# Moving the squares and RMS scales of a fused attention and SwiGLU kernel ahead of its loads, and leaving all engines but TensorE to a list scheduler

## The chip, the core and the metric

One core of one Trainium2 chip. The time is the device time of one execution in microseconds (us). A run's state is noted: it is called slow here when it is over 1.5% above the fastest run of the same kernel, and fast runs are compared with fast runs. The profiled span is about 1.7 us shorter than the reported time of the same execution.

Engines are named as in the profile: PE is TensorE (matmuls and transposes), PEld its weight loads, DVE VectorE, ACT ScalarE, POOL GpSimd, SP SyncE.

## What is computed

```python
# q, k, v: [8, 8, 576, 64] (batch, head, position, head dim); s: [8, 8, 576]
scores = (1 / 8) * q @ k^T + min(-(cum[i] - cum[j]), 0)   # cum = cumsum(max(s, 0)); causal
x = softmax(scores) @ v                                   # then [batch * position, 512]
xn = x / sqrt(mean(x * x) + 1e-6) * rms_g                 # RMS norm of each token
out = (silu(xn @ w_gate) * (xn @ w_val)) @ w_out          # 512 -> 1536 -> 512, 4608 tokens
```

## The kernel before

There are eight batches of 576 tokens in the attention, and nine chunks of 512 tokens in the feed-forward network (FFN). The kernel's main loop alternates them. `attention(b)` has eight units (a pair of heads and a part of the positions each). `ffn1(c)` is the gate and value matmuls of chunk c: twelve groups of 16 matmuls of 256 columns (8 of 512 in the later chunks), each into one of two PSUM buffers `psD`, followed by Silu on ACT and a product on DVE (`H_sb`). The second product, `ffn2_steps(c)`, is woven into the next attention. Three more words: a pack is a DVE copy that reorders a loaded q or k of batch 0 or 1 for its transposes; weighting v is POOL's product of v with the decay weights; a mask is POOL's instruction that makes `E` causal. Where an engine is said to stand, it is idle until something it waits for is done.

`ffn1` also takes fillers: small jobs with a place between 0 and 1, issued between its groups. In the kernel before they include the end of the previous attention: squares of blocks 2 to 4 of `x_blk` (ACT, with sums), the RMS scale `al` from those sums (POOL), the scaling (DVE) and the transposes into `psX` (PE).

```python
def att_square(a, tb):                                    # ACT
    nc.scalar.activation(out=sq_scr[:, 0:DM], in_=a.x[:, tb, :], func=AF.Square,
                         accum_out=a.ss[:, tb : tb + 1])
def att_alpha(a, t0, t1):                                 # POOL
    ... al = (ss / DM + 1e-6) ** -0.5 ...
def att_scale(a, tb):                                     # DVE
    ... a.x[:, tb, :] *= al[:, tb] ...
def att_out(a, tb):                                       # PE: x_blk -> psX; DVE: psX * g -> xnT
    ...
def tail_fillers(a, lo, hi):
    fns = [lambda tb=tb: att_square(a, tb) for tb in (2, 3, 4)]
    fns += [lambda: att_alpha(a, 2, 5)]
    fns += [lambda tb=tb: (att_scale(a, tb), att_out(a, tb)) for tb in (2, 3, 4)]
    return spread(fns, lo, hi)

def attention(b, filler, lead, each):
    ... # units; each: PE scores -> ACT exp (E) -> POOL causal mask -> PE psAV -> DVE x_blk
    ... # squares, al and scale of blocks 0 and 1 after units 4 and 6
    return a

with tc.manual_schedule():          # every engine runs in program order
    ... # loads and preparation of batch 0 (cut)
    a = attention(0, iter(()), (0, 0, 0), 0)
    load_runs(1, 0)                 # k of batch 1, issued by POOL
    load_runs(1, 1)                 # q of batch 1
    load_w(2, 0, 6)                 # w_out in two halves
    load_w(2, 6, 12)
    load_v(1, nc.gpsimd)            # v of batch 1, five loads
    for c in range(NCH):
        fillers = []
        if c < B:
            fillers += tail_fillers(a, 0.0, 0.25 if c == 0 else 0.4)
        ... # preparation of batch c + 1: packs (DVE), transposes, norms (ACT), v weighting (POOL)
        if c + 2 < B:
            for w in range(2):      # ten POOL issues: k and q of batch c + 2
                fillers.append((0.1, lambda b=c + 2, w=w: load_kq(b, w)))
            fillers.append((0.1, lambda b=c + 2: load_v(b, nc.sync)))
        if c == B:
            check_decay()           # checks of the input's range, before the last FFN
            check_all()
        Ht = ffn1(c, quarters if c == 0 else halves if c < 4 else whole, fillers)
        fl = ffn2_steps(c, Ht)
        if c + 1 < B:
            a = attention(c + 1, fl, (8, 4, 6), 3)
        else:
            for _ in fl:
                pass
... # a slow general path for inputs that fail the checks (cut)
```

## Time and profile before

| | before |
|---|---|
| time, us | 505.26 median of 2 runs (503.77 to 506.76) |
| profiled span, us | 504.7 |
| PE busy | 395.9 us, 78% of the span |
| PE waiting at `psX` for scaled `x_blk` | 77.5 us, 25 times, the longest 32.4 |
| mean granted PE clock | 0.925 of full speed |

First the page of the kernel before: busy time by engine, and the span in 40 equal slices of 12.6 us (a digit is tenths of busy time; PEclk is the granted clock in tenths).

```profile
PE 395.9 (78%) x3083; PEld 226.9 (45%) x3083; DVE 230.7 (46%) x461; ACT 215.1 (43%) x351; POOL 172.3 (34%) x267
...
PE   3740068697799779986998699959995999697995
...
PEclk9985559999899989998999899989998999998898
DMA  9999950019701980199019901990110011002002
```

PE works 78% of the time, and in slices 4 and 5 (counted from 1, 37.9 to 63.1 us) it does nothing at all, while the DMA engines are full (digit 9; 189 GB/s over these 25 us). The clock digit is 5 there and in the slice after. Who made PE wait is in the list of PE's waits (what it waited for: total us, times, longest):

```profile
PE psX L330 <- DVE x_blk L323: 77.5, 25, 32.4
PE psT L201 <- DVE xnT L191: 7.8, 7, 1.7
```

Most of it is one cause: transposes of `x_blk` that wait for the scaling on DVE (77.5 of the 108.8 us in which PE is not busy). The timeline of PE in the first FFN shows the long one (columns: start, duration, what; in brackets the idle time before it and what ended it):

```profile
31.34 1.04 PE L345 MATMUL psD<-xnT,wv_sb 128*128 128x256 bf16 x8
64.78 0.61 PE L330 MATMUL psX<-ident_bf,x_blk 128*128 128x128 bf16 x4 [32.40 <-DVE x_blk L323]
65.18 1.91 PE L345 MATMUL psD<-xnT,wg_sb 128*128 128x256 bf16 x8
```

PE stops at 32.4 and goes on at 64.8. The scaling waited for `al` on POOL, as DVE's timeline shows:

```profile
63.59 1.13 DVE L323 TENSOR_SCALAR x_blk<-x_blk,al 128x512 bf16<-128x512 bf16 x1 [29.00 <-POOL al L320]
```

POOL's timeline tells why `al` came so late:

```profile
29.18 2.68 POOL L118 DMA_DIRECT2D v_nat<-in_v_dram  x3
35.22 0.89 POOL L118 DMA_DIRECT2D v_nat<-in_v_dram  x1 [3.37 <-DMA wv_sb<-in_moe_w_val_dram]
...
43.93 0.89 POOL L105 DMA_DIRECT2D k_nat<-in_k_dram  x1 [3.86 <-DMA xnT<-in_q_dram]
...
59.88 2.43 POOL L105 DMA_DIRECT2D q_nat<-in_q_dram  x3 [0.36 <-DMA v_nat<-in_v_dram]
62.39 0.20 POOL L318 TENSOR_SCALAR al<-ss 128x3 f32<-128x3 f32 x1
```

POOL issues 19 loads between attention 0 and `al` (L318): k, q, two halves of w_out, five of v, then five each of k and q of batch 2. From the fourth load of v on it stands before nearly every one until an earlier load has landed. In the lines shown that is the eighth before it: the first `k_nat`, the tenth of the row, is released by the second, `in_q_dram`, after 3.86 us. The issue itself takes only 0.9 us, and its end in the record is not the landing of the load: the issue of 0.77 us for q of batch 1 landed 16.4 us after its start.

In later stages the same chain is shorter. In the second FFN, PE's timeline reads:

```profile
121.82 1.04 PE L345 MATMUL psD<-xnT,wv_sb 128*128 128x256 bf16 x8
125.50 0.61 PE L330 MATMUL psX<-ident_bf,x_blk 128*128 128x128 bf16 x4 [2.64 <-DVE x_blk L323]
125.90 1.91 PE L345 MATMUL psD<-xnT,wg_sb 128*128 128x256 bf16 x8
...
130.92 0.40 PE L330 MATMUL psX<-ident_bf,x_blk 128*128 128x128 bf16 x4 [1.68 <-DVE x_blk L323]
```

PE waits 2.64 and 1.68 us (a third wait, of 1.68, ends at 134.74). After the first, the matmuls run at about half speed: eight matmuls of 256 columns take 1.91 us and not 1.04. After the two waits of 1.68 us they take 1.04 and 1.05.

### The profile page before, as it was taken

The page shows a single profiled execution, that of the slowest core. Times are in us where ns is not written, and L with a number is a line of the kernel's source. Part 1 is how long each engine was busy: PE and PEld are TensorE (multiplying, and loading weights), DVE is VectorE, ACT ScalarE, POOL GpSimd, SP SyncE. Part 2 cuts the span into 40 slices and gives each one's busy share as a digit, 9 for nine tenths or more (in the row PEclk, how much of TensorE's full clock was granted, in tenths as well). Part 3 has the DMA queues.
Part 4 walks back from the last instruction along what each step waited for, and adds up shares of the span by engine and source line. Part 5 has one row for each costly group of instructions (what it writes and reads, how often), then busy time and mean ns, then how long its engine had stood idle before and what let it go on. Part 6 is the DMA issues. An engine that isn't in the chain of part 4 may idle for free.

```text
span 504.7 us, 7722 instructions
## 1 busy us (share of the span) xinstructions
PE 395.9 (78%) x3083; PEld 226.9 (45%) x3083; DVE 230.7 (46%) x461; ACT 215.1 (43%) x351; POOL 172.3 (34%) x267
## 2 busy tenths in 40 slices
PE   3740068697799779986998699959995999697995
PEld 2530047545584558455844254425442544243442
DVE  6730035565336634563355435643564356433331
ACT  2830006583257425751565156615652566120220
POOL 8651540049204930393039403940224022000000
PEclk9985559999899989998999899989998999998898
DMA  9999950019701980199019901990110011002002
GB/s 151 199 197 195 183 26 0 2 43 153 78 0 43 144 88 2 43 129 101 1 43 121 109 0 44 113 117 1 38 46 1 0 44 44 0 1 83 1 2 88
DMA packets 97803, 33.75 MB, mean 67 GB/s; under 512 B 85856, under 2 KB 92512, under 8 KB 97760
## 3 DMA queue, kind: packets, MB, share of 16 engines
q0 software_dynamic: 63840, 16.52, 34.5%
q1 hardware_dynamic: 33920, 16.67, 14.0%
q8 instruction: 26, 0.43, 0.3%
q14 instruction: 17, 0.14, 0.1%
HBM read 37.90 MB, written 9.44 MB: 94 GB/s over the span
## 4 chain that ended last, share of the span: by engine, by line
PE 57%; DMA 12%; POOL 10%; DVE 9%; ACT 8%; issue 4%; SPq 0%; ACTq 0%; POOLq 0%
PE psD L345 35%; PE psO L373 11%; DMA v_nat<-in_v_dram 8%; PE psT L211 4%; PE psX L330 3%; DMA xnT<-in_k_dram 3%; DVE H_sb L352 3%; ACT S_sb L351 3%; DVE x_blk L323 2%; POOL al L320 2%; POOL q_nat L105 2%; PE psAV L301 2%; ACT E L277 2%; POOL E L279 2%; PE psD L272 2%
## 5 line engine op out<-in xcount | busy, mean ns | idle before, releaser
L351 ACT ACTIVATE S_sb<-psD 128x512 bf16<-128x512 f32 x108 | 64.3, 595 | 240.1 <-PE psD L345 239.7
L352 DVE TENSOR_TENSOR H_sb<-S_sb,psD 128x512 bf16<-128x512 bf16 x108 | 74.2, 687 | 165.1 <-ACT S_sb L351 165.1
L345 PE MATMUL psD<-xnT,wg_sb 128*128 128x256 bf16 (+1 forms) x624 | 121.9, 335 | 0.0
L345 PE MATMUL psD<-xnT,wv_sb 128*128 128x256 bf16 (+1 forms) x624 | 118.3, 327 | 0.0
L279 POOL TENSOR_SCALAR_AFFINE_SELECT E<-E 128x512 bf16<-128x512 bf16 x64 | 41.1, 642 | 213.1 <-ACT E L277 212.9
L373 PE MATMUL psO<-wout_sb,H_sb 128*128 128x512 bf16 x432 | 107.4, 379 | 0.0
L345 PEld LDWEIGHTS <-wv_sb 128*128 128x128 bf16 x624 | 64.1, 103 | 38.0 <-issue 5.3
L330 PE MATMUL psX<-ident_bf,x_blk 128*128 128x128 bf16 x160 | 17.4, 238 | 77.6 <-DVE x_blk L323 77.5
L345 PEld LDWEIGHTS <-wg_sb 128*128 128x128 bf16 x624 | 60.1, 104 | 30.9 <-issue 2.8
L277 ACT ACTIVATE E<-psD 128x1024 bf16<-128x1024 f32 x64 | 63.6, 1023 | 8.0 <-PE psD L272 7.7
L373 PEld LDWEIGHTS <-H_sb 128*128 128x128 bf16 x432 | 36.9, 98 | 34.9 <-issue 3.0
L330 PEld LDWEIGHTS <-x_blk 128*128 128x128 bf16 x160 | 10.6, 104 | 90.6 <-DVE x_blk L323 87.6
L378 DVE COPY osb<-psO 128x512 f32<-128x512 f32 x36 | 24.8, 688 | 29.1 <-PE psO L373 29.1
L301 PE MATMUL psAV<-vw,E 128*128 128x65 bf16 x576 | 32.3, 199 | 6.2 <-POOL E L279 4.3
L237 POOL TENSOR_TENSOR vw<-v_nat,wT 128x512 bf16<-128x512 f32 (+1 forms) x35 | 35.5, 1044 | 0.0
L301 PEld LDWEIGHTS <-E 128*128 128x128 bf16 x576 | 23.6, 100 | 20.1 <-POOL E L279 10.7
L323 DVE TENSOR_SCALAR x_blk<-x_blk,al 128x512 bf16<-128x512 bf16 x40 | 18.9, 489 | 29.8 <-POOL al L320 29.3
L306 DVE TENSOR_TENSOR x_blk<-psAV,rZ 128x256 bf16<-128x256 f32 (+1 forms) x64 | 31.4, 491 | 2.2
L334 DVE TENSOR_TENSOR xnT<-psX,g_sb 128x512 bf16<-128x512 bf16 (+1 forms) x40 | 24.8, 636 | 14.3 <-PE psX L330 13.7
L105 POOL DMA_DIRECT2D k_nat<-in_k_dram x30 | 25.8, 880 | 12.2 <-DMA wout_sb<-in_moe_w_out_dram 7.7
L272 PE MATMUL psD<-QT,KT 64*128 64x256 bf16 (+2 forms) x320 | 26.7, 266 | 0.9 <-ACT E L277 0.9
L105 POOL DMA_DIRECT2D q_nat<-in_q_dram x30 | 25.4, 901 | 1.6 <-DMA v_nat<-in_v_dram 1.6
(80 smaller groups left out, 289.9 us busy)
## 6 DMA issues: line engine op xcount, KB each, us to landing
out_dram<-osb SPq DMA_DIRECT2D x36, 256.0 KB, 2.0
v_nat<-in_v_dram SPq DMA_DIRECT2D x24, 256.0 KB, 9.7
k_nat<-in_k_dram POOLq DMA_DIRECT2D x24, 128.0 KB, 4.5
q_nat<-in_q_dram POOLq DMA_DIRECT2D x24, 128.0 KB, 7.9
v_nat<-in_v_dram POOLq DMA_DIRECT2D x8, 256.0 KB, 16.0
wg_sb<-in_moe_w_gate_dram POOLq DMA_DIRECT2D x2, 768.0 KB, 14.8
wv_sb<-in_moe_w_val_dram POOLq DMA_DIRECT2D x2, 768.0 KB, 18.6
wout_sb<-in_moe_w_out_dram POOLq DMA_DIRECT2D x2, 768.0 KB, 22.7
```

Source lines behind the costliest of these rows:

```text
L105: nc.gpsimd.dma_start(out=dst[0:n, b % 2, sc, :, :], in_=src[b, :, sc * 128 : sc * 128 + n, :].rearrange("h p d -> p h d"))
L237: eng.tensor_tensor(out=vw[0:n, sc, :, 0:64], in0=v_nat[0:n, b % 2, sc, :, :], in1=wb.unsqueeze(2).to_broadcast([n, H, D]), op=ALU.mult)
L272: nc.tensor.matmul(st[:, j, c0 : c0 + q1 - q0], lhsT=KT[rs, hp, kb * 128 : kb * 128 + 128], rhs=QT[rs, hp, q0:q1], start=(i == 0), stop=(i ...
L277: nc.scalar.activation(out=E, in_=st, func=AF.Exp, scale=0.125)
L279: nc.gpsimd.affine_select(out=diag, in_=diag, pattern=[[0, 4], [1, 128]], compare_op=ALU.is_ge, fill=0.0, base=0, channel_multiplier=-1)
L301: nc.tensor.matmul(AV[:, j, qb - q0, :], lhsT=E[:, j, c0 : c0 + 128], rhs=vw[:, kb, h, :], start=(j == 0 and i == 0), stop=(j == 1 and i = ...
L306: nc.vector.tensor_tensor(out=a.x[:, q0 : q0 + nq, hp * 128 : (hp + 1) * 128].rearrange("p t (j d) -> p j t d", j=2), in0=AV[:, :, :, 0:64 ...
L330: nc.tensor.matmul(X[:, cc, :], lhsT=a.x[:, tb, cc * 128 : (cc + 1) * 128], rhs=ident_bf, is_transpose=True, start=(cc == 0), stop=(cc == ...
L345: nc.tensor.matmul(P[:, j, i * n : (i + 1) * n], lhsT=w[:, cc, fb * 128 : (fb + 1) * 128], rhs=xnT[:, cc, t0 + o : t0 + o + n], start=(i = ...
L351: nc.scalar.activation(out=sl, in_=P[:, 0, :], func=AF.Silu)
L352: nc.vector.tensor_tensor(out=Ht[:, f0 : f0 + m, o : o + n], in0=sl.rearrange("p (i n) -> p i n", i=m), in1=P[:, 1, :].rearrange("p (i n) ...
L373: nc.tensor.matmul(O, lhsT=Ht[:, fb, tb * 128 : (tb + 1) * 128], rhs=wout_sb[:, fb, :], start=(fb == 0), stop=(fb == FB - 1))
```

## The change

The intent is to take the chain squares, scale factor, scaling out of the FFN: its squares, `al` and scaling of blocks 2 to 4 are issued at the end of `attention`, ahead of the next loads, and only the transposes stay in the FFN. In the same step the program order is kept on PE alone. On the other engines a list scheduler now orders the instructions at build time (it changes their order on each engine, not what they do).

```diff
-    def tail_fillers(a, lo, hi):
-        fns = [lambda tb=tb: att_square(a, tb) for tb in (2, 3, 4)]
-        fns += [lambda: att_alpha(a, 2, 5)]
-        fns += [lambda tb=tb: (att_scale(a, tb), att_out(a, tb)) for tb in (2, 3, 4)]
-        return spread(fns, lo, hi)
+    def tail_fillers(a, steps):
+        return [(p, lambda tb=tb: att_out(a, tb)) for p, tb in zip(steps, (2, 3, 4))]
@@ attention
             take(filler, each)
+        for tb in (2, 3, 4):
+            att_square(a, tb)
+        att_alpha(a, 2, 5)
         if each:
             for tb in (0, 1):
                 att_out(a, tb)
             for _ in filler:
                 pass
+        for tb in (2, 3, 4):
+            att_scale(a, tb)
         return a
@@
-    with tc.manual_schedule():
+    with tc.manual_schedule(engines={mybir.EngineType.PE}):
@@
-                fillers += tail_fillers(a, 0.0, 0.25 if c == 0 else 0.4)
+                fillers += tail_fillers(a, (0.08, 0.16, 0.24) if c == 0 else (0.16, 0.25, 0.33))
```

## The prediction

> **What bounds the kernel now.** 505.26 us; TensorE (PE) is busy 395.9 of 504.7 us (part 1 of the page). By the list of waits PE waits 77.5 us in 25 gaps at the transposes into psX for the scaled x_blk. One gap is 32.4 us (timeline, 32.4 to 64.8): the RMS scale of blocks 2 to 4 (POOL al) stands on POOL behind the next batches' loads, whose issues wait for earlier loads to land; DMA is saturated there (about 190 GB/s in the stage table). In each later stage (50 to 51 us) the same chain costs PE about 2.6+1.7+1.7 us, and afterwards a group of 16 matmuls at the half clock takes 3.3 instead of 1.8 us.
>
> **What the change does.** No work is added or removed. The order of instructions shows:
> 1. Squares and scale of blocks 2 to 4 stand before the FFN; in the first batch the scale now follows three of the v loads instead of all remaining issues. In later stages it follows the v weighting (4 blocks at 1.01 us) and precedes the k/q loads, which go to the end of the FFN.
> 2. New hazard: on VectorE (DVE) the pack of q of batch 1 stands in attention 0, before unit 5's normalisation. It waits for a load that landed at 43.2 us (issue 26.8 + 16.4), behind the same saturated queue. [...] so attention 0 stands until 43 to 44.
> 3. In later attentions the scaling of blocks 0 and 1 stands before unit 5's normalisation and waits for POOL, which has one weighting block (1.01 us) more between the masks. Loss.
> 4. After the attention ACT does 3 squares, two norms (1.2 us each) and the table load (1.28 us) before the first Silu. The third FFN group waits for that and for H_sb behind xnT on DVE.
> 5. The decay checks leave the last FFN's front.
>
> **Sum, from durations in the trace.**
> - Start: q lands 43.5; packs, units 5 and 6, scales, transposes, unit 7 to 49.3; group 0 (cold, 3.7) 53; Silu, square, scale on POOL (behind one 0.9 us issue) 56.5; group 1 from 57.3; group 3 from 66 (before 72.5); nine groups at 1.8, eight transposes at 0.43, a cold group: FFN 0 ends about 87.5, before 99.6. Its pack-to-transpose waits (4 x 1.5 us) vanish. Gain 12.
> - Stages 1 to 5: the transposes' waits and the cold group (about 7) go; attention +2.0, one PE wait of about 1.8 before group 2: gain about 3.2 each, 16. Stages 6 and 7: 3.2 + 2.7.
> - Last FFN: PE waits 3.6 us for the checks, 1.6 remain: gain 2.
>
> Total about 36: **predicted 469 us**, 80% range 459 to 481. Faster by over 2%: 0.96; within 2%: 0.03; slower: 0.01.
>
> **What would show it.** The 32.4 us gap becomes one of about 20 us (24 to 44), released by DVE packing q; then about 4 us at the first psX. FFN 0 ends at 86 to 89. Stages 1 to 5 last about 48 us; their FFN starts 2 us later after the attention's start, PE's waits for x_blk near zero, about 1.8 at group 2.
>
> **What would make it wrong.** q landing much earlier or later; ACT's norms delaying the first Silu until PE goes cold in every stage (1.5 us each, 10 in all); masks delayed by k/q issues at the start of an attention; the clock.

That attention 0 stands until 43 to 44 was my assumption; the trace of the kernel after shows such a stand (below). The sum comes to about 36 us.

## The result, and the profile after

| | before | after |
|---|---|---|
| time, us (2 runs each) | 505.26 (503.77 to 506.76) | 457.78 (457.10 to 458.46) |
| profiled span, us | 504.7 | 455.4 |
| PE busy, us | 395.9 | 379.5 |
| mean granted PE clock | 0.925 | 0.989 |

The ratio is 0.906, 95% interval 0.8931 to 0.9189. Ratios here are the mean time of one kernel's fast runs over the mean of the other's fast runs of the same rounds, so they are not quite the ratios of the medians quoted. The kernel is 47 us faster, predicted were 36: the time fell 1.2 us below the range's lower end of 459.

The same lines of the page, after (a slice is now 11.4 us):

```profile
PE 379.5 (83%) x3083; PEld 222.8 (49%) x3083; DVE 225.7 (50%) x461; ACT 217.3 (48%) x351; POOL 171.4 (38%) x267
...
PE   1640599988988899879986998889988998999994
...
PEclk9999989999999999999999999999999999999998
DMA  8999999450092409850594019100110011002002
```

One hole is left in PE's line (slice 4, 34 to 46 us). The clock digits are 8 and 9 throughout, but this record is too kind just after the hole. By stretches (columns: window, its length, busy time and number of instructions of PE, PEld, DVE, ACT, POOL; granted clock, DMA share, GB/s):

```profile
46.00:52.00 6.00, 5.10 (x36) 3.69 (x36) 2.79 (x7) 2.28 (x5) 0.00 (x0) 1.00 1.22 218
56.00:60.00 4.00, 3.69 (x25) 2.90 (x26) 2.48 (x7) 2.48 (x6) 4.00 (x5) 0.58 0.90 124
```

From 46 to 52 us a clock of 1.00 is recorded, and yet eight matmuls take 1.90 us there, as at half speed (PE's timeline below, 48.56). The record and the durations disagree here, and I go by the durations. PE's waits:

```profile
PE psX L330 <- DVE x_blk L323: 22.8, 2, 18.7
PE psD L345 <- DVE H_sb L352: 11.5, 6, 1.9
PE psAV L301 <- DVE x_blk L306: 10.0, 7, 1.5
...
PE psAV L301 <- POOL E L279: 7.1, 5, 1.7
```

The 77.5 us at `psX` fell to 22.8, of which 18.7 are one wait. Three rows that are new or larger stand out: waits for `H_sb` before an FFN group (11.5), for `x_blk` (10.0) and for the mask `E` (7.1) before a `psAV`. The timeline of PE in the start:

```profile
26.37 1.50 PE L301 MATMUL psAV<-vw,E 128*128 128x65 bf16 x24
46.55 1.03 PE L330 MATMUL psX<-ident_bf,x_blk 128*128 128x128 bf16 x8 [18.68 <-DVE x_blk L323]
...
48.56 1.90 PE L345 MATMUL psD<-xnT,wg_sb 128*128 128x256 bf16 x8
...
56.30 0.60 PE L330 MATMUL psX<-ident_bf,x_blk 128*128 128x128 bf16 x4 [4.14 <-DVE x_blk L323]
56.70 1.91 PE L345 MATMUL psD<-xnT,wg_sb 128*128 128x256 bf16 x8
...
62.24 1.03 PE L345 MATMUL psD<-xnT,wg_sb 128*128 128x256 bf16 x8
```

PE now stands inside attention 0, from 27.87 to 46.55, and then 4.14 us for `al`. DVE's timeline shows what the first stand is:

```profile
43.99 0.36 DVE L191 COPY xnT<-xnT 96x768 bf16<-96x768 bf16 x1 [17.28 <-DMA xnT<-in_q_dram]
44.27 0.18 DVE L305 RECIPROCAL rZ<-psAV 128x6 f32<-128x6 f32 x1
```

The scheduler put the packing of q of batch 1 (L191) before attention 0's normalisation of unit 5 (L305, L306), and it waits for its load. The instructions behind it did not pass: PE had ended its `psAV` matmuls at 27.87, and yet the reciprocal that reads them (L305) started only behind the pack, at 44.27. DVE was idle for 17.28 us meanwhile.

To see where the 49.3 us of span lie, I cut both spans at the first FFN matmul and the first `psO` matmul of each chunk, read from PE's timeline:

| stretch, us | before | after | difference | predicted |
|---|---|---|---|---|
| start to first FFN matmul | 27.67 | 48.56 | +20.9 | |
| FFN 0 | 71.93 | 31.45 | -40.5 | |
| together: start to end of FFN 0 | 99.60 | 80.01 | -19.6 | -12 |
| attentions 1 to 5 | 89.25 | 103.07 | +13.8 | +10 |
| FFN 1 to 5 | 166.67 | 136.53 | -30.1 | -26 |
| attentions and FFN 6 and 7 | 94.98 | 86.58 | -8.4 | -5.9 |
| FFN2 of chunk 7 with the checks, last FFN | 37.49 | 32.52 | -5.0 | -2 |
| tail | 16.71 | 16.69 | 0.0 | |
| sum | 504.7 | 455.4 | -49.3 | -36 |

FFN 1 to 5 gained 6.0 us each, 33.3 to 27.3 in the mean: the waits for `x_blk` and the cold matmuls (those at about half speed, 1.91 us for eight of 256 columns) are gone; in FFN 1 to 5 of the kernel after, every such row takes 1.02 to 1.05 us. The attentions lost: attention 2 takes 22.1, numbers 3 to 5 take 20.6, numbers 1, 6 and 7 take 19.0, all of them 17.9 before. In attention 2 PE's timeline reads:

```profile
131.29 0.39 PE L272 MATMUL psD<-QT,KT 64*128 64x256 bf16 x4
133.40 0.36 PE L301 MATMUL psAV<-vw,E 128*128 128x65 bf16 x6 [1.72 <-POOL E L279]
```

and POOL's in the same stretch:

```profile
124.87 4.31 POOL L105 DMA_DIRECT2D k_nat<-in_k_dram  x5 [23.29 <-ACT S_sb L351]
129.14 3.54 POOL L105 DMA_DIRECT2D q_nat<-in_q_dram  x4
132.62 0.72 POOL L279 TENSOR_SCALAR_AFFINE_SELECT E<-E 128x512 bf16<-128x512 bf16 x1
```

The first mask (L279) starts as the ninth POOL issue of k and q loads for a later batch ends; the scheduler put them in front. Its input was ready some 1.5 us before (ACT's three exps began at 130.04 and take 0.95 each). PE waits 1.72 us.

In the FFN, the new wait comes from ACT: in FFN 2 the squares, two norms (L231) and the loading of the Silu table stand before the first Silu, and the third group waits for a free `psD`:

```profile
151.17 1.04 PE L345 MATMUL psD<-xnT,wv_sb 128*128 128x256 bf16 x8
...
154.34 0.93 PE L345 MATMUL psD<-xnT,wg_sb 128*128 128x256 bf16 x7 [1.91 <-DVE H_sb L352]
```

```profile
150.50 1.06 ACT L231 ACTIVATE sq_scr<-k_nat 128x1024 bf16<-128x1024 bf16 x1
...
151.67 1.28 ACT L351 ACT_TABLE_LOAD   x1
152.97 1.09 ACT L351 ACTIVATE S_sb<-psD 128x512 bf16<-128x512 f32 x2
```

So the profile suggests that the new source order gains much, and that the scheduler's order gives part of it back: at the pack of q (DVE), at the masks (POOL), at the norms (ACT). That is a reading, and the experiments test it.

### The profile page after: what moved, and what is told of

It is laid out like the page before. It is cut to its first block, busy times and chain, and to the rows that moved or that the text cites. A ratio compares the mean times of both kernels' runs of the same rounds, so it can differ in the third digit from the quotient of the medians.

```text
span 455.4 us, 7760 instructions
## 1 busy us (share of the span) xinstructions
PE 379.5 (83%) x3083; PEld 222.8 (49%) x3083; DVE 225.7 (50%) x461; ACT 217.3 (48%) x351; POOL 171.4 (38%) x267
## 4 chain that ended last, share of the span: by engine, by line
PE 51%; issue 11%; POOL 11%; ACT 10%; DVE 8%; DMA 7%; POOLq 0%; ACTq 0%
PE psD L345 33%; PE psO L373 10%; DMA xnT<-in_q_dram 6%; POOL E L279 5%; PE psT L211 3%; DVE x_blk L306 3%; ACT sq_scr L313 3%; ACT E L277 2%; ACT sq_scr L231 2%; PE psD L272 2%; DVE x_blk L323 1%; POOL vw L237 1%; POOL q_nat L105 1%; POOL al L320 1%; DVE osb L378 1%
## 5 line engine op out<-in xcount | busy, mean ns | idle before, releaser
L351 ACT ACTIVATE S_sb<-psD 128x512 bf16<-128x512 f32 x108 | 63.8, 596 | 130.0 <-PE psD L345 128.6
L345 PE MATMUL psD<-xnT,wg_sb 128*128 128x256 bf16 (+1 forms) x624 | 113.5, 318 | 11.7 <-DVE H_sb L352 11.5
L345 PE MATMUL psD<-xnT,wv_sb 128*128 128x256 bf16 (+1 forms) x624 | 112.7, 316 | 0.0
L345 PEld LDWEIGHTS <-wv_sb 128*128 128x128 bf16 x624 | 61.8, 99 | 33.4
L345 PEld LDWEIGHTS <-wg_sb 128*128 128x128 bf16 x624 | 57.2, 99 | 39.3 <-issue 12.5
L279 POOL TENSOR_SCALAR_AFFINE_SELECT E<-E 128x512 bf16<-128x512 bf16 x64 | 41.3, 653 | 85.2 <-ACT E L277 84.9
L313 ACT ACTIVATE sq_scr<-x_blk 128x512 bf16<-128x512 bf16 x40 | 25.1, 627 | 51.0 <-DVE x_blk L306 50.5
L301 PE MATMUL psAV<-vw,E 128*128 128x65 bf16 x576 | 30.8, 202 | 18.1 <-DVE x_blk L306 10.0
L301 PEld LDWEIGHTS <-E 128*128 128x128 bf16 x576 | 23.5, 102 | 31.9 <-DVE x_blk L306 13.5
L330 PE MATMUL psX<-ident_bf,x_blk 128*128 128x128 bf16 x160 | 16.1, 227 | 25.6 <-DVE x_blk L323 22.8
L306 DVE TENSOR_TENSOR x_blk<-psAV,rZ 128x256 bf16<-128x256 f32 (+1 forms) x64 | 31.3, 489 | 1.9
L305 DVE RECIPROCAL rZ<-psAV 128x4 f32<-128x4 f32 (+1 forms) x64 | 11.7, 183 | 36.8 <-PE psAV L301 36.8
L323 DVE TENSOR_SCALAR x_blk<-x_blk,al 128x512 bf16<-128x512 bf16 x40 | 14.9, 408 | 28.1 <-POOL al L320 28.1
L330 PEld LDWEIGHTS <-x_blk 128*128 128x128 bf16 x160 | 11.3, 101 | 34.0 <-DVE x_blk L323 23.5
## 6 DMA issues: line engine op xcount, KB each, us to landing
wv_sb<-in_moe_w_val_dram POOLq DMA_DIRECT2D x2, 768.0 KB, 18.8
wout_sb<-in_moe_w_out_dram POOLq DMA_DIRECT2D x2, 768.0 KB, 22.6
```

What stands on the lines that cost most here:

```text
L279: nc.gpsimd.affine_select(out=diag, in_=diag, pattern=[[0, 4], [1, 128]], compare_op=ALU.is_ge, fill=0.0, base=0, channel_multiplier=-1)
L301: nc.tensor.matmul(AV[:, j, qb - q0, :], lhsT=E[:, j, c0 : c0 + 128], rhs=vw[:, kb, h, :], start=(j == 0 and i == 0), stop=(j == 1 and i = ...
L306: nc.vector.tensor_tensor(out=a.x[:, q0 : q0 + nq, hp * 128 : (hp + 1) * 128].rearrange("p t (j d) -> p j t d", j=2), in0=AV[:, :, :, 0:64 ...
L345: nc.tensor.matmul(P[:, j, i * n : (i + 1) * n], lhsT=w[:, cc, fb * 128 : (fb + 1) * 128], rhs=xnT[:, cc, t0 + o : t0 + o + n], start=(i = ...
L351: nc.scalar.activation(out=sl, in_=P[:, 0, :], func=AF.Silu)
```

## The experiments

The theory: the moved squares and scales bring the whole gain, and the list scheduler costs time in three separate places, one for each engine. The rival: both halves belong together, and the scheduler brings part of the gain (for example, by placing `al` and the loads better than the source does). Each run is compared with the kernel before on the same chip (medians of before: 504.80, 504.54 and 503.99 us in the three sessions). The variants of the scheduler are one line each. They are correct, as all runs here are.

### The two halves of the change

The new source with every engine in program order:

```diff
-    with tc.manual_schedule(engines={mybir.EngineType.PE}):
+    with tc.manual_schedule():
```

> The changed source (squares and scales in front of the loads), program order kept on all engines. Theory M (all of the gain comes from the moved squares and scales; the list scheduler takes part of it back, by packing q inside attention 0 and by issuing loads in front of the masks): 433 us (428 to 440), faster than the changed kernel by about 25; FFN 0 starts at about 28 us as in the kernel before instead of 48.6, attentions last 17.9 us as before, FFNs 27 to 28. Rival R (the scheduler's order brings most: packs, peaks and checks out of the way): 475 to 490, slower than the changed kernel.

Measured: 421.78 us median of five runs, 420.40 of the three fast ones; ratio of the fast runs 0.8332 (0.8295 to 0.8369). That is 37 us faster than the kernel after, fast runs with fast runs. The runs fell in two groups, 420.1 to 421.8 and 427.0 to 427.3 (slow); this comes up again below. The run takes the edit of the source as a whole: that it is the chain moved ahead of the loads, and not the new places of the transposes, is read from PE's waits for scaled `x_blk` (77.5 us before, 4.0 in e1's second profile); no run took the two apart.

The old source with the scheduler:

```diff
# in the kernel before
-    with tc.manual_schedule():
+    with tc.manual_schedule(engines={mybir.EngineType.PE}):
```

> The source of before, order kept on PE only. On POOL the scale of blocks 2 to 4 of batch 0 stays behind all loads, but in later stages the scheduler puts it in front of them. Theory M: 465 us (459 to 475): the stall at the start ends at about 65 us as before, FFN 0 ends near 88 us, later stages as in the changed kernel. Rival R': the source part is needed in every stage, then 485 to 500.

Measured: 477.33 us (476.40 to 477.77, four runs); ratio 0.9451 (0.9422 to 0.9480). I had expected 465. In later stages the scheduler alone does move `al` ahead of the loads (after attention 1 `al` of blocks 2 to 4 starts at 108.20 and the loads of k at 134.52; before, the loads were first) and so heals part of the old order. In the first batch it does not: `al` starts at 61.86, as late as before (62.39). PE still waits 30.1 us for scaled `x_blk`; 18.1 of them are the same stand in attention 0 as in the kernel after, the other 12.0 are for this `al`.

What follows: the halves overlap. From the old source, the scheduler gains 27 us. From the new source, it loses 37 us. The rival is right about the first and wrong about the kernel at hand: with the source order mended, the scheduler of all four engines costs far more than it gains. In this sense the theory, "the whole gain is the source's", stands; how much of the 47 us one ascribes to each half depends on which is put in first.

### Which engine's order costs what

One engine more is given back its program order, from the kernel after:

```diff
-    with tc.manual_schedule(engines={mybir.EngineType.PE}):
+    with tc.manual_schedule(engines={mybir.EngineType.PE, mybir.EngineType.DVE}):    # e3
+    with tc.manual_schedule(engines={mybir.EngineType.PE, mybir.EngineType.Pool}):   # e4
```

> The changed kernel with program order kept on DVE too. Theory M: the 18.7 us wait in attention 0 is DVE standing at the pack of q, so it goes: FFN 0 starts at 28 us, PE then waits at the first psX until about 38, FFN 0 ends at 68 to 70; then the masks of attention 1 stand behind the k/q loads of batch 3 on POOL until about 78, so only 4 to 8 us remain of it: 450 us (445 to 455). Rival: attention 0 stands for another reason (DMA or POOL), FFN 0 starts at 45 or later and the time stays at 456 to 460.

> The changed kernel with program order kept on POOL too. Theory M: the extra time of attentions 2 to 5 (20.6 to 22.1 us against 19.0 for 1, 6, 7) is the k/q loads issued on POOL in front of the masks; with them back in the FFN these attentions last 19 us or less, 7 to 9 us less in all, and as the scheduler then places the pack of q after attention 0, FFN 0 starts before 32 us: 437 us (431 to 444). Rival (DVE's and ACT's order make the attentions long): attentions 2 to 5 stay above 20 us.

Measured: 448.75 us with DVE in order (447.37 to 452.22, ratio 0.8872, 0.8842 to 0.8902) and 437.08 with POOL in order (436.35 to 440.63, ratio 0.8642, 0.8615 to 0.8668). Both are as expected in time; in e3 partly by luck, since FFN 0 was expected to end at 68 to 70 and ended at 79.2. With DVE in order, FFN 0 starts at 28.98 and not at 48.56: the stand of 18.7 us was DVE's order. But FFN 0 then takes 50.2 and not 31.5 us, so the start as a whole gains only 0.8 us: in program order DVE does the packs of batch 1 shortly before PE needs them, PE waits four times for them (1.68, 1.84, 5.09 and 2.04 us) and 5.15 us for `al`, and the granted clock over FFN 0 is 0.77. This profile is the slowest of e3's five runs, 3.5 us above their median, and the wait of 5.09 belongs to a long pack of the kind told below; what the start gains without it, no profile shows. With POOL in order FFN 0 ends at 63.8 us, and attentions 2 to 5 take 18.8 to 19.1. Attention 1 takes 24.2, however: POOL weights v of batch 1 (65.45 to 70.48) only after it has issued all loads of k and q of batch 2, and the masks come behind it.

Next, all but one engine in order:

```diff
+    with tc.manual_schedule(engines={mybir.EngineType.PE, mybir.EngineType.DVE, mybir.EngineType.Pool}):          # e6: ACT scheduled
+    with tc.manual_schedule(engines={mybir.EngineType.PE, mybir.EngineType.Activation, mybir.EngineType.Pool}):   # e7: DVE scheduled
```

> The changed kernel with program order kept on PE, DVE and POOL: against e1_source_only only ACT's order (and SP's) is the scheduler's. Theory A (the wait of 1.9 us at the third group of each FFN is ACT: two norms stand before the first Silu): FFNs 27.2 to 27.6 us as in the changed kernel, attentions 17.7 to 17.9 as in e1; 430 to 433 us, about 10 more than e1_source_only. Rival D (it is H_sb behind xnT on DVE): FFNs 25.7, time within 2 us of e1_source_only.

> The changed kernel with program order kept on PE, ACT and POOL: against e1_source_only only DVE's order (and SP's) is the scheduler's. Theory A: FFNs 25.7 as in e1. The scaling of blocks 0 and 1 in front of later normalisations costs 0.5 to 1.2 us per attention (18.3 to 19.0), the early decay checks save 5.0 us at the last FFN (11.8 + 20.7 against 14.0 + 23.6), the early packs of batch 1 shorten FFN 0 from 42 to about 33 us while attention 1 then waits for its v weights as in e4_pe_pool (24 us). Together about e1_source_only: 418 to 425 us. Rival D: FFNs above 27.

Measured: with ACT alone scheduled 437.91 us (437.67 to 441.87, ratio 0.8674, 0.8612 to 0.8736), some 17 more than the fast runs with all in order; I had expected 430 to 433. In its profile the two packs took 4.35 us at 64.49, the slow case of the two that are told below, so its start (72.9 us) is to be compared with e1's slow run (70.2 us) and not with the column beside it. With DVE alone scheduled 416.33 (414.37 to 417.56, ratio 0.8226, 0.8170 to 0.8281), the fastest up to then and below the 418 to 425 expected: attention 1 took 19.2 us and not 24.

| stretch, us | after: all but PE scheduled | e3: POOL, ACT scheduled | e4: DVE, ACT scheduled | e6: ACT scheduled | e7: DVE scheduled | e1 again: none scheduled |
|---|---|---|---|---|---|---|
| start to end of FFN 0 | 80.0 | 79.2 | 63.8 | 72.9 | 61.5 | 63.3 |
| attention 1 | 19.1 | 18.5 | 24.2 | 18.7 | 19.2 | 17.9 |
| attention 2 | 22.1 | 19.3 | 18.8 | 17.9 | 17.9 | 17.9 |
| attentions 3 to 5, mean | 20.6 | 19.9 | 19.0 | 17.9 | 17.9 | 17.9 |
| FFN 1 to 6, mean | 27.3 | 27.4 | 27.5 | 27.6 | 25.7 | 25.7 |
| FFN2 of chunk 7, checks | 11.8 | 13.9 | 11.8 | 14.0 | 11.8 | 13.9 |

("e1 again" is the second profile of e1, below. The starts of e3 and e6 hold a long pack. The order of SP, which issues loads and stores, is the scheduler's in all columns but that of e1 again.) The table gives each engine its part:

- ACT's order costs 1.9 us in each of FFN 1 to 5 (27.4 to 27.2 in e6, 25.5 to 25.3 in e1 again). Every column with ACT scheduled has 27 to 28 us in the mean, both without it have 25.7. In e6, where ACT alone is scheduled, PE's waits show the same row as after (11.5 us there):

```profile
PE psD L345 <- DVE H_sb L352: 11.6, 6, 2.0
```

- POOL's order costs 1.4 to 3.3 us in each of attentions 2 to 5: they are long where POOL is scheduled (after, e3) and 17.9 to 19.1 where it is in order. In both runs ACT was scheduled too. Another 0.9 to 1.2 us are a matter of their own: they are there when DVE and ACT are both scheduled (e4), and gone with either alone (e6, e7). They go with PE's seven waits for `x_blk` before a `psAV` (10.0 us after and in e4; no such row in e3, e6 and e7): DVE has the scaling of blocks 0 and 1, which waits for POOL's `al` (2.14 us at 143.47 in the kernel after), before a normalisation. This is item 3 of the prediction.
- DVE's order alone costs nothing in the attentions (I had expected 0.5 to 1.2 us each: a miss) and gains 2.1 us at the checks, part of which it takes off the critical path, and 1.4 in the last FFN (22.1 to 20.7), where the matmuls then start at full speed (four of 512 columns take 1.04 us, and 1.89 in the kernel before). The 17.3 us stand of DVE at the pack of q is not in e7, where FFN 0 starts at 29.75, nor in e3 and e4: it goes when either DVE or POOL is given its order back. (In every run that has it, ACT was scheduled too.) Why the scheduler places the pack so early only then, no run shows.

So "one separate place for each engine" was too simple. ACT's cost in the FFN stands alone (e6); POOL's in the attentions was seen only beside ACT's order, as no run scheduled POOL alone; the stand in the start and the 0.9 to 1.2 us in the attentions need at least two engines' orders together.

### Does the start hang on q's landing?

The load of q is issued before that of k, in the kernel after:

```diff
-        load_runs(1, 0)
         load_runs(1, 1)
+        load_runs(1, 0)
```

> The changed kernel with the load of q of batch 1 issued before that of k (two lines swapped). If attention 0 stands for the landing of q and for nothing else, q lands about 4.5 us earlier (39.5 instead of 44.0), FFN 0 starts at about 44.1 instead of 48.6 and the time falls by 3.5 to 4.5 us to 453.5. Rival (what holds attention 0 and FFN 0 is the total of the loads, or POOL): the start of FFN 0 may move, the start of FFN 1 (99.1 us) does not.

Measured: 454.56 us (453.44 to 455.19, ratio 0.8983, 0.8926 to 0.9039). DVE's pack of q came 4.0 us earlier than the 43.99 of after:

```profile
39.95 1.16 DVE L191 COPY xnT<-xnT 96x768 bf16<-96x768 bf16 x4 [15.17 <-DMA xnT<-in_q_dram]
```

FFN 0 started 2.7 us earlier (expected 4.5) and FFN 1 1.8 us earlier. The rest went to the order behind it: all four packs (1.16 us) now stand in one row before unit 5, and PE has twelve more `psAV` matmuls to do after the stand. So the landing of q does set the end of that stand. The time fell by 3.2 us between medians, somewhat less than the 3.5 to 4.5 expected; the two intervals of the ratios overlap, so this rests on the traces.

### The two groups of e1

The profiled run of e1 is one of the 427 us group, which is slow. In it two packs of batch 1 took 5.65 us together, 5.25 of them the first; usually each takes 0.3. The same kernel again, for a second profile:

> e1 word for word, for a second profile: e1's runs fell in two groups, 420 to 422 and 427, and its profiled run was of the second. In that one two packs of batch 1 took 5.65 us on VectorE while POOL weighted v. Theory: the groups are that meeting of the packs with the weighting. A run at 420 to 422 should show those packs at about 0.3 us each and FFN 0 near 37; a run at 427 should show them long again with FFN 0 at 42. Rival: packs are alike and the difference lies elsewhere (clock, loads).

Measured: 418.90 us, one run (its time belongs with the faster group). FFN 0 takes 35.3 us, against 42.3 in the slow run of e1. The spans, 417.1 and 425.3, differ by 8.2 us, so this is most of it. DVE and POOL in the slow run (e1):

```profile
60.73 5.65 DVE L191 COPY xnT<-xnT 96x768 bf16<-96x768 bf16 x2
```

```profile
60.71 5.04 POOL L237 TENSOR_TENSOR vw<-v_nat,wT 128x512 bf16<-128x512 f32 x5
```

and in the fast one (e1 again):

```profile
60.63 0.61 DVE L191 COPY xnT<-xnT 96x768 bf16<-96x768 bf16 x2
```

```profile
61.53 5.03 POOL L237 TENSOR_TENSOR vw<-v_nat,wT 128x512 bf16<-128x512 f32 x5
```

In the slow run POOL began weighting v at 60.71. The first pack, recorded from 60.73, ended only after POOL's five instructions (65.75), at 65.98, and the second at 66.38. PE waited 6.38 us for them. In the fast run the packs ran at 60.63 to 61.24 and the weighting began at 61.53. The expectation holds: whether the packs or the weighting come first by a fraction of a us decides over some 7 us. Two other profiles have the long packs: e3 (4.58 us from 64.03, beside a weighting that began at 62.95) and e6 (4.35 us). So the two profiles differ in this meeting; the lower mean clock of the slow one (0.972, against 0.989) goes with the matmuls at about half speed after PE's longer wait (eight took 1.91 us at 66.49, and 1.04 in the fast run). The two groups should not have been read as one. What makes the packs long is not shown: POOL came first by 0.02 us in e1 and by 1.08 in e3, but no run took it apart. In the kernel before, a DVE scaling beside the same POOL row (it started at 63.59, the row at 63.53) took only 1.13 us, against 0.35 otherwise; what decides between the two cases, no run shows.

### Is there a version that beats both?

With all engines in order (e1's line), three edits against what was left: the checks as four fillers of the last FFN, the packs of batch 1 earlier, its norms later.

```diff
-                check_decay()
-                check_all()
+                fillers += [(0.1, check_decay), (0.2, check_a), (0.3, check_b), (0.5, check_c)]
@@ prep_fillers
-                         for h in range(0, H, 2) for w in range(2)], lo - 0.06, hi - 0.06)
-        f += spread([lambda i=i: prep_norm(b, i) for i in range(3)], lo, hi)
+                         for h in range(0, H, 2) for w in range(2)], lo - 0.16, hi - 0.16)
+        f += spread([lambda i=i: prep_norm(b, i) for i in range(3)],
+                    0.9 if b < 2 else lo, hi)
```

> e1_source_only with the decay checks split into four pieces that stand among the groups of the last FFN, the packs of batch 1 two FFN groups earlier and its norms after the packs. Theory: 5.0 us from the checks (att 7 to FFN 8 11.8, FFN 8 20.7), FFN 0 without the packs' waits at 32 to 34 us, but attention 1 then waits for the weighted v until about 67 us, so FFN 1 starts at 80 to 84 us: 411 to 416 us, faster than both kernels and than e1_source_only; and no run about 6 us longer than the others, since no pack on DVE falls into POOL's v weighting.

Measured: 415.78 us (414.40 to 418.00, ratio 0.8223, 0.8167 to 0.8278). FFN 0 ended at 57.5 us and FFN2 of chunk 7 with the checks took 10.4, but attention 1 took 23.4 us and not 17.9. POOL weighted v of batch 1 only after ten issues of k and q. The next run moves the weighting forward:

```diff
# from e10
         load_w(2, 0, 6)
-        load_w(2, 6, 12)
         load_v(1, nc.gpsimd)
+        load_w(2, 6, 12)
@@ the weighting of v of batch 1 at 0.2 to 0.5 (was 0.8), the q loads of batch 2 at 0.6 (was 0.1)
```

> e10 with the loads of v of batch 1 moved ahead of the second half of wout, the v weighting of batch 1 ahead of the loads of q of batch 2, all engines in program order. Theory: attention 1 of e10 took 23.4 us because the weighting stood on POOL behind all ten k and q issues (60.97 to 66.3) and the masks behind it. Here the weighting should run at about 52 to 57 and the last q issue end at about 61.5, so the first mask comes about 4.5 us earlier and attention 1 takes 18.5 to 20; all else as in e10. Expected 411 to 412. Rival (attention 1 is slow because of loads landing or the cold clock after its gap, not POOL's order): 415 to 416 as e10. Risk: the second half of wout lands after 58.8 and FFN2 of chunk 0 waits instead.

Measured: 415.54 us median of four runs; the two fast ones 411.02 and 412.83, the two slow 418.25 and 418.75. What made the two slow runs slow, no profile shows. In the profile FFN 0 ended at 55.3, and attention 1 still took 22.6. I had expected 18.5 to 20: a miss. POOL:

```profile
58.83 4.26 POOL L105 DMA_DIRECT2D q_nat<-in_q_dram  x5
63.07 1.84 POOL L285 TENSOR_SCALAR_AFFINE_SELECT E<-E 128x512 bf16<-128x512 bf16 x3
```

The weighting is early now, but the q issues end at 63.09 and not at the expected 61.5, and the first mask starts as they end. PE's timeline in attention 1:

```profile
57.90 0.59 PE L379 MATMUL psO<-wout_sb,H_sb 128*128 128x512 bf16 x2 [1.19 <-DMA wout_sb<-in_moe_w_out_dram]
63.80 0.36 PE L307 MATMUL psAV<-vw,E 128*128 128x65 bf16 x6 [1.97 <-POOL E L285]
```

Of the 4.7 us that attention 1 takes beyond 17.9, POOL's order is 1.97. Another 1.19 is a wait for the second half of w_out, whose load now comes later (the risk named in the expectation), and most of the rest is matmuls at a lower speed after these gaps: two rows of three `psO` matmuls take 1.42 and 1.44 us, and not 0.81. So I moved part of the hold from one job to another, and added a new one.

The same source with DVE scheduled:

```diff
# from e11
-    with tc.manual_schedule():
+    with tc.manual_schedule(engines={mybir.EngineType.PE, mybir.EngineType.Activation, mybir.EngineType.Pool}):
```

> The same source as e11, with VectorE alone ordered by the list scheduler (as in e7). e7 and e10 gave the same time; in e7 the scheduler's order of VectorE cost nothing. If it costs nothing here either: within 2 us of e11 (410 to 414). If e7's gains were only those that e10 makes by hand (checks, earlier packs), nothing is added.

Measured: 414.63 us (413.19 to 417.00, ratio 0.8218, 0.8158 to 0.8277), just above the 410 to 414 expected. e7, e10, e11 and e12 are not told apart by these runs. The median of each is below that of the kernel after by 41 us or more; the simplest is e7, which is the kernel after with two engine names added.

## Why the prediction was right or wrong

**Right:** the direction (faster at 0.96); the mechanism of most parts. The gap of 32.4 us became one of 18.7, released by DVE behind the pack of q, which began at 43.99 (predicted 43 to 44), and the waits of `psT` for packs (7.8 us before) are gone. A wait of 4.14 us at the first `psX` followed (predicted about 4). Stages 1 to 5, attention and FFN together, gained 30.1 - 13.8 = 16.3 us (predicted 16), though both parts were larger than predicted; the errors cancelled, and that is luck.

**Wrong: the size, and most of it in one term, the start ("FFN 0 ends about 87.5, before 99.6 ... Gain 12").** It ended at 80.01: a gain of 19.6. Up to group 1 the sum was right within 0.6 us (predicted 57.3, measured 56.70). Two steps after it failed:

- "Group 3 from 66": it started at 62.24. I took the second Silu to stand behind norms of batch 1 that wait for all packs of k (the prediction does not write this out). ACT's timeline shows that the first of them began after the first pack already, and the Silu at 60.89:

```profile
57.94 1.06 ACT L231 ACTIVATE sq_scr<-xnT 96x1024 bf16<-96x1024 bf16 x1 [0.73 <-DVE xnT L191]
...
60.89 0.57 ACT L351 ACTIVATE S_sb<-psD 128x512 bf16<-128x512 f32 x1
```

- "Nine groups at 1.8, eight transposes at 0.43, a cold group" makes 21.5 us; measured from 62.24 to 80.01 are 17.8. A group takes 1.75 us in pitch. A transpose takes 0.25 in pitch: its six small matmuls have a busy time of 0.42, which overlaps the next matmuls (psT at 70.97, the next group at 71.23). 9 x 1.75 + 8 x 0.25 = 17.75 accounts for all of it, so there was no cold group: PE had stood 0.3 us at most before group 3.

Each is worth 3.7 us (the first with the 0.6 us gained up to group 1), together 7.5 of the 13 us that were missing. The rest: stages 6 and 7 gained 8.4 and not 5.9, since their attentions lost 1.2 us each and not 2.0, and their FFN gained 5.2 and 5.5; the checks and the last FFN gained 5.0 and not 2. There I counted the wait for the checks alone; the last FFN also fell from 23.5 to 20.7 us, because before, its first matmuls after that wait ran at half speed (four of 512 columns took 1.89 us, after 1.04).

**Named only as a risk, and it came true:** "masks delayed by k/q issues at the start of an attention". Item 1 has these loads go to the end of the FFN. They began there (at 124.87 in FFN 1) but ran on to 134.0, well into attention 2, which starts at 126.44. It cost attentions 2 to 5 some 1.6 to 3.1 us each, beyond the 1.2 us of attentions 1, 6 and 7.

**Not seen at all:** how much the scheduler takes away. The prediction listed its hazards one by one as part of a sum. It didn't ask what the sum would be without the scheduler. Against the second profile of e1 (span 417.1), the kernel after loses 16.7 us up to the end of FFN 0, 15.9 in the attentions and 9.4 in FFN 1 to 7, and gains 3.7 at the checks and the end: 38.3.

## What to carry to other kernels

A chain of small instructions through several engines belongs ahead of anything that can stand, above all ahead of load issues on the engine that computes one of its links: here `al` came behind 19 of them, and PE waited 32.4 us. When a change has two halves, run each alone: here one half gave 84 us and the other took back 37, and the sum looked like a success. Handing the order of an engine to a scheduler should be decided engine by engine, and a load's consumer should not be placed before work that is ready: here DVE stood 17.28 us at such a pack, with ready work behind it.
